# A new order for the opening and the hand-over, and gathers issued in twos behind a result

## The chip, the cores and the metric

The kernel runs on one core of one Trainium2 chip. The metric is the device time of one execution in microseconds (us). Three runs of the kernel before took 702.27, 704.57 and 707.97 us; the median is 704.57 us.

The core has five engines with a queue of instructions each: TensorE (PE; its weight loads are shown as PEld), VectorE (DVE), ScalarE (ACT), GpSimd (POOL) and SyncE (SP), which here only starts transfers. Sixteen DMA engines move the data.

## The reference

Attention within hash buckets, and a mixture of experts behind it (numpy, float32):

```python
q_bucket = sum((q @ proj > 0) * 2**bit); k_bucket likewise      # 4 batches, 8 heads, 768 tokens, 64 wide
scores   = q @ k.T / sqrt(64), -1e9 where the buckets differ
x        = softmax(scores) @ v            # 3072 tokens of 512
logits   = x @ w_gate;  e = argmax(logits)            # 8 experts
out[tok] = softmax(logits)[e] * sigmoid(x @ w_output_gate)[e] * (relu(x @ w1[e]) @ w2[e])
```

The products are made in three float32r parts (high x high, low x high, high x low), so each operand comes as a high tile and a low tile (`xh`/`xlo`, `hh`/`hl`, `w1h`/`w1l`).

## The kernel before, in words

**Attention.** The work runs in 192 steps of a query tile of one head. A step makes scores (TensorE, `ps_s`), clamps them and takes the row extreme (VectorE), exponentiates (ScalarE), divides by the row sum (GpSimd), transposes and multiplies with `v`. The order on each engine is the order of the code: whole blocks are planned by step with `plan` and `block`. `first_heads` (from line 596) is the opening: it splits the first two heads' `q` and `k` into high and low parts before any scores can start. SP writes each head's halves and its bucket bits into place (`spread`).

**Routing and hand-over.** The last batch's routing runs on VectorE beside the first products of the *leading* expert, the fullest one up to then: `fill(f)` makes one of eight slices of relu(x w1) for that expert's first 256 rows, `low()` its low part. `add_pair` adds the last heads' logits, `best`/`choose`/`ranks`/`hot`/`table`/`entries` make the table of which token stands at which place of which expert. With it `lead_slots` and `indices` give row numbers.

**Gathers.** Row numbers go to GpSimd, which starts *indirect* DMAs: `gather` fetches 128 whole rows (`xg`, line 324), `gather_part` a quarter (`xq`, line 365: 128 pieces of 512 bytes), `scatter` writes 128 result rows (line 424). The list `parts` holds the quarter gathers that are still to be issued; `gather_some(m)` issues the next m. An `xq` tile has 4 buffers.

**Experts.** For each expert in order of size (index r, from 0, the leading one), `up` makes two slices at a time: 24 products into one of two `ps_s` buffers, then ScalarE's relu writes `hh` (line 404) and VectorE writes `hl` (line 405); the buffer is free for the next but one slice after that. Then come the products with w2 (`all_rows` or `down`). The turned rows of the next expert are prepared meanwhile (`turned`: VectorE transposes `xq` into `xt`, line 374). For r = 0 the rows 0 to 255 have been worked on ahead (`EARLY`), so its loop takes rows 256 to 511 (`x0`, filled by two `turn` calls).

The order of the engines' queues follows the code, except that pieces of the second recorded region (from line 1310) can be drawn into gaps of the first.

Of the kernel before, what the change touches and what calls it, by code (L numbers as in the profile page):

```python
# [65 lines left out]
def lsh_attention_then_moe(  # L66
# [452 lines left out]
    with ExitStack() as actx:  # L519
# [76 lines left out]
        def first_heads(t):  # L596

            qk, qh, ql, kh, kl = tiles(0, 0)
            qk1, qh1, ql1, kh1, kl1 = tiles(0, 1)
            bb = bits_of(0, 0)  # L600
            first = slice(0, HS)
            pp = ps_m.tile([P, HS], F32, name="ps_m")
            for m in range(2):
                nc.tensor.matmul(pp[m * D:(m + 1) * D], pj[:, 0:D], qk[:, m * HS:(m + 1) * HS], start=True, stop=True)
            nc.scalar.copy(kh, qk[:, KEYS])
            nc.vector.tensor_scalar(qh[DOWN, KEYS], qk[UP, first], -0.125, 0.0, ALU.mult, ALU.add)
            nc.scalar.activation(qh[:, first], qk[:, first], AF.Copy, scale=-0.125)
            signed(t)
            nc.gpsimd.tensor_scalar(kh1, qk1[:, KEYS], 1.0, 0.0, ALU.mult, ALU.add)
            nc.vector.tensor_tensor(kl, qk[:, KEYS], f32(kh), ALU.subtract)  # L610
            nc.scalar.activation(qh1[:, first], qk1[:, first], AF.Copy, scale=-0.125)
            bt = hp.tile([P, HS], BF16, name="bt", bufs=2)
            nc.vector.tensor_scalar(bt, pp, 0.0, set0, ALU.is_gt, ALU.is_equal)
            nc.vector.scalar_tensor_tensor(ql[:, first], qk[:, first], -0.125, f32(qh[:, first]),
                                           ALU.mult, ALU.subtract)
# [4 lines left out]
            for h in range(2):  # L620
                r = D + 32 * h
                nc.gpsimd.tensor_scalar(bb[h * D:h * D + 2 * NB, S:S + HS], bt[r:r + 2 * NB], 1.0, 0.0,
                                        ALU.mult, ALU.add)
            project(0, ps_a.tile([P, HS], F32, name="ps_a"), (1,))

            for n in range(2):
                for h in range(2):
                    c = (n ^ h) * HS
                    nc.scalar.activation(bb[h * D:h * D + 2 * NB, c:c + HS], bt[32 * n:32 * n + 2 * NB],
                                         AF.Copy, scale=PEN)  # L630
            nc.gpsimd.tensor_tensor(kl1, qk1[:, KEYS], f32(kh1), ALU.subtract)
            for m in (1, 0):
                spread_bits(0, 1, m)
            for h in (1, 0):
                spread_bits_half(0, 1, h)

        def second_low():
            split_lo(0, 1, 0)
            for h in (1, 0):
                spread_half(0, 1, h)  # L640
# [14 lines left out]
        def split_late(j):  # L655
            st = pairs[1]
            q = gp.tile([P, S // 32, 32], F32, name="xb", bufs=1).rearrange("p a b -> p (a b)")[:, 0:HS]
            nc.gpsimd.tensor_scalar(q, st["qk"][j][:, 0:HS], -0.125, 0.0, ALU.mult, ALU.add)
            nc.gpsimd.tensor_tensor(st["ql"][j][:, 0:HS], q, f32(st["qh"][j][:, 0:HS]), ALU.subtract)
# [145 lines left out]
        def routing(b):  # L805
# [28 lines left out]
            def add_pair(hf, i):  # L834
                pm = ps_m.tile([P, 3, 32], F32, name="ps_m")
# [134 lines left out]
        for g in range(NP):  # L970
# [15 lines left out]
            elif g == 1:  # L986
                plan(0, lambda: split_hi(1, 0), lambda: split_lo(1, 0, 1, nc.gpsimd))
                plan(2, second_low, lambda: load_v(0), lambda: load(2))
# [75 lines left out]
        def order():  # L1064
# [14 lines left out]
            for i in range(1, E):  # L1079
                load_expert(idi, i)  # L1080
            for i in (0, 2, 1):
# [80 lines left out]
        with tc.manual_schedule(engines=MANUAL | {mybir.EngineType.SP}):  # L1162
            t = signs()
# [16 lines left out]
            turn_idle(12)  # L1180
            first_heads(t)
            turn_idle(1)
# [32 lines left out]
            for s in range(PER, NSTEP + LAG, 2):  # L1215
                k = s % PER
                both = range(s, s + 2)
                for x in both:
                    if x < NSTEP:
                        live[x] = scores(x)  # L1220
                        raw.append(x)
                    if x == PER:
                        project(1)
# [48 lines left out]
            low()  # L1272
            r["add_pair"](1, lp)
# [4 lines left out]
            rows(NP - 1, 1, False)  # L1278
# [14 lines left out]
            r["table"]()  # L1293
            low()
            r["entries"]()
            gid0 = lead_slots(EARLY)
# [3 lines left out]
    with tc.manual_schedule(engines=MANUAL):  # L1300
        pick = slot_picks()
        xg = [gather(gid0[:, a:a + 1]) for a in range(EARLY)]
        order()
        gid, sid = indices(mp, tacc)
        xgs = {(1, a): (gather(gid[:, 1, a:a + 1])[0], chunks(1)[a]) for a in range(WHOLE)}
# [16 lines left out]
        for a in range(WHOLE, NCH):  # L1322
            fetch(a, 1)
        x0 = new_x0()
        for c in range(EARLY):
            py = ps_s.tile([P, 2, 512], F32, name="ps_s")[:, 0]
            for f in range(0, NFB, 2):
                down_rows(c, CH, w2s, hs, py, [f, f + 1])
                if c and f in (2, 4):
# [9 lines left out]
        for r in range(E):  # L1339
# [29 lines left out]
            for fp in range(NFB // 2):  # L1369
# [6 lines left out]
                split()  # L1376
                gather_some(2)
# [5 lines left out]
            def hook(k, a, cc):  # L1383
# [8 lines left out]
                gather_some(2)  # L1392
# [123 lines left out]
```

## Time and profile before

| | us |
|---|---|
| median of three runs | 704.57 |
| the profiled execution | 704.21 |
| its span, first to last instruction | 702.4 |
| TensorE busy in the span | 681.2 |
| VectorE, ScalarE, GpSimd busy | 475.1, 434.6, 414.9 |

All times of rows are from the start of the span. "Idle before" is how long the engine stood still before a row, and the name behind the arrow is what ended it; "issue" means nothing that the profile shows, "remote" an event that it can't put to an engine of the core. Of a row of products the length is modelled, so their pace is read from the distance of their starts.

### The profile page before, as it was taken

Reading aid. Unit: us, or ns where it says so; the run is one execution under the profiler, and the core shown is the slowest. Engines: PE = TensorE matmul, PEld = TensorE weight load, DVE = VectorE, ACT = ScalarE, POOL = GpSimd, SP = SyncE. Lnnn points to the kernel's source line nnn. Section 1 sums busy time; section 2 is a strip of 40 time slices with the busy share of each in tenths; the row PEclk is TensorE's granted clock in tenths of the full one; section 3 lists DMA queues with packets and bytes.
Section 4 is the critical chain, followed back from the end, with each engine's and each line's share of the span. In section 5 each row is a group of like instructions: output and inputs, shape, how many; then the busy total and the mean of one; then the engine's idle time right before and its main releaser. Section 6 shows DMA issues by size and latency. Waiting matters only on the chain. (4 is left out here: it accounts for less than half of the span.)

```text
span 702.4 us, 17340 instructions
## 1 busy us (share of the span) xinstructions
PE 681.2 (97%) x6537; PEld 540.3 (77%) x6537; DVE 475.1 (68%) x1058; ACT 434.6 (62%) x889; POOL 414.9 (59%) x553
## 2 busy tenths in 40 slices
PE   8999999999999999999999968999999999899997
PEld 4667676766766676767676958889999999888996
DVE  6878887889887888878878704563747464545640
ACT  6788998889888988898985112531515252343241
POOL 5877766577756778567985473444272727274003
PEclk9999999999999999999999987999999999999999
DMA  4644454354434444424453223734657576665332
GB/s 145 176 122 102 128 129 97 80 136 120 108 108 96 119 109 123 122 60 90 133 176 67 71 70 113 247 109 146 217 188 248 191 229 201 190 216 185 132 90 84
DMA packets 96724, 96.07 MB, mean 137 GB/s; under 512 B 57967, under 2 KB 76967, under 8 KB 96632
## 3 DMA queue, kind: packets, MB, share of 16 engines
q1 hardware_dynamic: 79704, 72.88, 36.9%
q0 software_dynamic: 5312, 13.25, 5.3%
q10 hardware_dynamic: 11616, 8.75, 4.3%
q8 instruction: 54, 0.88, 0.5%
q14 instruction: 38, 0.31, 0.1%
HBM read 63.77 MB, written 17.50 MB: 116 GB/s over the span
## 5 line engine op out<-in xcount | busy, mean ns | idle before, releaser
L725 POOL TENSOR_SCALAR sc<-sc,rsum 128x768 f32<-128x768 f32 x191 | 170.9, 911 | 77.3 <-ACT pts L761 37.5
L706 DVE TENSOR_SCALAR_CACHE_REDUCE sc<-ps_s 128x768 f32<-128x768 f32 x192 | 176.4, 954 | 23.2 <-PE ps_s L703 21.9
L714 ACT ACTIVATE sc<-sc,mn 128x768 f32<-128x768 f32 x192 | 178.8, 951 | 2.9 <-DVE sc L706 2.7
L703 PE MATMUL ps_s<-kh,qhl 64*128 64x384 f32 x768 | 149.2, 403 | 0.5 <-DMA qhl<-qhl 0.5
L404 ACT ACTIVATE hh<-ps_s 128x256 fp32r<-128x256 f32 (+8 forms) x40 | 29.1, 727 | 173.2 <-PE ps_s L394 96.2
L772 PE MATMUL ps_a<-pts,vt 128*64 128x384 f32 x768 | 131.2, 491 | 0.0
L365 POOL DMA_INDIRECT xq<-x_dram,idx x86 | 91.5, 1064 | 33.3 <-issue 23.8
L761 ACT COPY pts<-ps_t 128x384 f32<-128x384 f32 x188 | 92.8, 495 | 24.2 <-PE ps_s L754 21.0
L394 PE MATMUL ps_s<-xh,w1h 128*128 128x256 f32 (+7 forms) x288 | 98.3, 341 | 9.5 <-DVE hl L405 9.3
L772 PEld LDWEIGHTS ps_a<-pts,vt 128*64 128x64 f32 x768 | 52.4, 137 | 66.8 <-issue 61.5
L394 PE MATMUL ps_s<-xh,w1l 128*128 128x256 f32 (+7 forms) x288 | 97.2, 337 | 1.7 <-issue 1.7
L394 PE MATMUL ps_s<-xlo,w1h 128*128 128x256 f32 (+7 forms) x288 | 97.4, 338 | 0.7 <-issue 0.7
L754 PEld LDWEIGHTS ps_t<-ident,sc 64*128 64x128 f32 x1140 | 81.8, 138 | 20.3 <-POOL sc L725 10.8
L405 DVE SCALAR_TENSOR_TENSOR hl<-ps_s,hh 128x256 fp32r<-128x256 f32 (+8 forms) x40 | 33.9, 848 | 92.6 <-ACT hh L404 73.3
L754 PE MATMUL ps_t<-ident,sc 64*128 64x64 f32 x1140 | 86.7, 223 | 0.0
L703 PEld LDWEIGHTS ps_s<-kh,qhl 64*128 64x128 f32 x768 | 76.6, 189 | 1.6 <-DMA qhl<-qhl 0.8
L394 PEld LDWEIGHTS ps_s<-xh,w1h 128*128 128x128 f32 x288 | 55.9, 194 | 14.0 <-DVE hl L405 10.9
L703 PE MATMUL ps_s<-kl,qhl 64*128 64x384 f32 x384 | 66.6, 334 | 0.0
L703 PE MATMUL ps_s<-bb 64*128 64x384 bf16 x384 | 65.1, 328 | 0.7 <-DMA bb<-bt 0.3
L380 POOL TENSOR_SCALAR xh<-xt 128x512 fp32r<-128x512 f32 (+5 forms) x21 | 11.9, 567 | 82.8 <-DVE xt L374 74.6
L394 PEld LDWEIGHTS ps_s<-xh,w1l 128*128 128x128 f32 x288 | 55.8, 194 | 2.7 <-issue 1.6
L394 PEld LDWEIGHTS ps_s<-xlo,w1h 128*128 128x128 f32 x288 | 55.8, 194 | 1.6 <-issue 0.5
(273 smaller groups left out, 1388.7 us busy)
## 6 DMA issues: line engine op xcount, KB each, us to landing
w_raw<-in_w_dram SPq DMA_DIRECT2D x31, 512.0 KB
qk<-in_qkT_dram SPq DMA_DIRECT2D x32, 384.0 KB
qhl<-qhl SPq DMA_DIRECT2D x62, 192.0 KB
xh<-in_w_dram SPq DMA_DIRECT2D x14, 512.0 KB
xlo<-in_w_dram SPq DMA_DIRECT2D x14, 512.0 KB
vt<-in_v_dram SPq DMA_DIRECT2D x16, 384.0 KB
x_dram<-xb SPq DMA_DIRECT2D x60, 96.0 KB
yt<-y_dram ACTq DMA_DIRECT2D x14, 256.0 KB
```

The lines of the kernel that those rows point to most:

```text
L365: nc.gpsimd.indirect_dma_start(out=xq[:, k * P:(k + 1) * P], out_offset=None, in_=x_dram.rearrange("n (a f) -> (n a) f", a=NB32), in_offse ...
L380: nc.gpsimd.tensor_scalar(xh, w[:, :, 0:n], 1.0, 0.0, ALU.mult, ALU.add)
L394: nc.tensor.matmul(ps, l, r, start=first and k == 0, stop=last and k == len(pairs) - 1)
L404: nc.scalar.activation(hh, ph, AF.Relu)
L405: return lambda: nc.vector.scalar_tensor_tensor(hl, ph, 0.0, f32(hh), ALU.max, ALU.subtract)
L703: nc.tensor.matmul(ss[:, h, 0:HS], q[rs, c:c + P], k[rs, 0:HS], start=(i == 0), stop=(i == 3))
L706: nc.vector.tensor_scalar(sc, ss[:, :, 0:HS], MASKED, None, ALU.min, ALU.min, accum_out=mn)
L714: nc.scalar.activation(pr, pr, AF.Exp, bias=mn, scale=-1.0, accum_out=sums[s // GROUP][:, k, 0:1])
L725: e.tensor_scalar(live[s0 + k], live[s0 + k], rs[:, k:k + 1], 0.0, ALU.mult, ALU.add)
L754: nc.tensor.transpose(trs[h][:, c], pr[r, c * P:(c + 1) * P], ident[r, r])
L761: (nc.vector.tensor_copy if h and s and (last or s % PER == 0 or s in (3, 5)) else nc.scalar.copy)(pts[:, :, t * P + h * hq:t * P + (h + 1 ...
L772: nc.tensor.matmul(st["av"][n * D:(n + 1) * D], st["v"][:, n if g else hf, c], blocks[hb][n][:, c], start=(c == 0), stop=(c == NT - 1))
```

## The change

The opening: TensorE's warm-up runs on a tile of zeros and is split around the first projection; ScalarE and VectorE make the parts of `q` before those of `k`; the low part of the second head's `q`, which VectorE made inside step 2 (`second_low`), is made by ScalarE and GpSimd in the opening. SP starts the bits of a half before its `q` parts, in every pair. The hand-over: the last pair's `add_pair` calls, the low parts of w1 and the last rows' transposes stand later, `low()` of slice 0 earlier, and `table`, `entries` and the row gathers behind the first two w2 products of chunk 0. The gathers: `pace` is a one-element GpSimd copy of a result, so that GpSimd waits until that result is there.

```diff
@@ first_heads
+            turn_idle(2)
+            nc.scalar.activation(qh[:, first], qk[:, first], AF.Copy, scale=-0.125)
+            nc.vector.tensor_scalar(qh[DOWN, KEYS], qk[UP, first], -0.125, 0.0, ALU.mult, ALU.add)
             nc.scalar.copy(kh, qk[:, KEYS])
...
+            q = scaled()
+            nc.scalar.activation(q, qk1[:, first], AF.Copy, scale=-0.125)
+            nc.gpsimd.tensor_tensor(ql1[:, first], q, f32(qh1[:, first]), ALU.subtract)
...
-        def second_low():
-            split_lo(0, 1, 0)
-            for h in (1, 0):
...
@@ spread
             for h in (1, 0):
+                spread_bits_half(g, j, h)
                 spread_half(g, j, h)
-                spread_bits_half(g, j, h)
@@ the opening's warm-up
-            turn_idle(12)
+            for i in range(8):
+                nc.tensor.matmul(idle[:, i % 3], blank, blank, start=True, stop=True)
+            turn_idle(1)
             first_heads(t)
-            turn_idle(1)
@@ hand-over
             for i, (p, hi) in enumerate(zip(w2p, early["w2h"] + [w2_round(ep, p, nc.scalar) for p in w2p[2:]])):
-                if i == 2:
-                    for cc in range(1, NCC):
-                        late_low(cc)
                 w2s += w2_low(ep, p, hi)
+                if i == 0:
+                    low()
             for c in range(NT):
                 weighted(2 * NP - 1, c)
-                if c == 0:
-                    rows(NP - 1, 0, False)
-                if c == 2:
-                    r["add_pair"](0, lp)
+            for cc in range(1, NCC):
+                late_low(cc)
             fill(1)
-            low()
-            r["add_pair"](1, lp)
+            for hf in range(2):
+                r["add_pair"](hf, lp)
...
@@ experts
-        for a in range(WHOLE, NCH):
-            fetch(a, 1)
+        def pace(x):
+            nc.gpsimd.tensor_copy(mp.tile([1, 1], F32, name="tick", bufs=2), f32(x))
+
         x0 = new_x0()
         for c in range(EARLY):
...
                 down_rows(c, CH, w2s, hs, py, [f, f + 1])
+                if c == 0 and f == 0:
+                    r["table"]()
+                    r["entries"]()
+                    gid0 = lead_slots(EARLY)
+                    xg = [gather(gid0[:, a:a + 1]) for a in range(EARLY)]
...
                 if c and f in (2, 4):
                     turn(xg[f // 2 - 1], x0, (f // 2 - 1) * CH)
+                    pace(x0[0][0:1, 0, (f // 2 - 1) * CH:(f // 2 - 1) * CH + 1])
+                    gather_some(2)
             send(0, c, CH, py, sid)
             if c == 0:
                 idx = slot_rows(tacc, pick)
-                gather_some(NCH * EARLY)
+            gather_some(2 - c)
@@ up, of each expert
                 split()
+                if r == 0:
+                    pace(hs[0][0:1, 2 * fp, 0:1])
                 gather_some(2)
@@ down, of each expert
-                gather_some(2)
+                if r or k % 2 == 0:
+                    gather_some(2 if r else 1)
```

GpSimd's queue from the end of the routing table to the middle of the second expert, before (`xg`, `xq`: gathered rows and quarters; `out_dram`: a scatter of results):

```order
L275 TENSOR_TENSOR t_rhs<-t_rhs,t_gl 128x192
L324 DMA xg<-x_dram,gid_8143 128x512 x2
L324 DMA xg<-x_dram,gid 128x512
L424 DMA out_dram<-yo,sid 3072x512
L365 DMA xq<-x_dram,idx 128x128 x8
L424 DMA out_dram<-yo,sid 3072x512
L365 DMA xq<-x_dram,idx 128x128 x13
L424 DMA out_dram<-yo,sid 3072x512
L365 DMA xq<-x_dram,idx 128x128 x4
L424 DMA out_dram<-yo,sid 3072x512
L380 TENSOR_SCALAR xh<-xt 128x4x128 x2
```

The same place now:

```order
L324 DMA xg<-x_dram,gid_8248 128x512 x2
L324 DMA xg<-x_dram,gid 128x512
L424 DMA out_dram<-yo,sid 3072x512
L365 DMA xq<-x_dram,idx 128x128 x2
L1325 COPY tick<-xh_8226 1x1
L365 DMA xq<-x_dram,idx 128x128 x2
L1325 COPY tick<-xh_8226 1x1
L365 DMA xq<-x_dram,idx 128x128 x2
L424 DMA out_dram<-yo,sid 3072x512
L365 DMA xq<-x_dram,idx 128x128
L1325 COPY tick<-hh 1x1
L365 DMA xq<-x_dram,idx 128x128 x2
```

The first eight quarter gathers stood in one row, and thirteen behind the second scatter. Now a copy that waits for a turned row (`xh`) or a relu (`hh`) stands after two, two and three of them; behind the last row shown come a copy, two gathers, two copies and four gathers.

VectorE's queue in the hand-over, from the last pair's low parts to the first step of the routing, before (`w1l`, `w2l`: low parts of weights; `lgt`: logits; `ot`: the last heads' result; `xb`: rows on their way to memory):

```order
L226 TENSOR_TENSOR w2l<-w2l,w2h 128x1024 x2
L1132 TENSOR_TENSOR w1l<-w_raw,w1h 128x512 x2
L1132 TENSOR_TENSOR w1l<-w_more,w1h 128x512
L226 TENSOR_TENSOR w2l<-w2l,w2h 128x1024 x2
L795 STREAM_TRANSPOSE xb<-ot 128x384
L840 TENSOR_TENSOR lgt<-lgt,ps_m 128x48
L775 COPY ot<-ps_a 128x384
L405 SCALAR_TENSOR_TENSOR hl<-ps_s,hh 128x256
L840 TENSOR_TENSOR lgt<-lgt,ps_m 128x48
```

and now:

```order
L226 TENSOR_TENSOR w2l<-w2l,w2h 128x1024
L405 SCALAR_TENSOR_TENSOR hl<-ps_s,hh 128x256
L226 TENSOR_TENSOR w2l<-w2l,w2h 128x1024 x3
L777 COPY ot<-ps_a 128x384
L1138 TENSOR_TENSOR w1l<-w_raw,w1h 128x512 x2
L1138 TENSOR_TENSOR w1l<-w_more,w1h 128x512
L843 TENSOR_TENSOR lgt<-lgt,ps_t 128x48
L843 TENSOR_TENSOR lgt<-lgt,ps_m 128x48
```

The copy of `ot`, on which the last logits wait, moved ahead of three low parts of w1, a transpose and a sum of logits.

## Rows read from the trace of the kernel before

**Rows 1.** The page: the span, and TensorE's busy time, share and instructions.
```profile
span 702.4 us, 17340 instructions
PE 681.2 (97%) x6537; PEld 540.3 (77%) x6537; DVE 475.1 (68%) x1058; ACT 434.6 (62%) x889; POOL 414.9 (59%) x553
```

**Rows 2.** Waits, whole span: engine, waits for, us in total, times, longest.
```profile
ACT hh L404 <- remote: 77.0, 7, 17.8
```

**Rows 3.** Waits from 400 to 435 us.
```profile
ACT hh L404 <- remote: 16.6, 2, 12.1
PE ps_s L394 <- DVE hl L405: 7.5, 1, 7.5
```

**Rows 4.** Timeline of TensorE, first expert: start, length, line, output and inputs, [idle before].
```profile
408.13 0.28 PE L394 MATMUL ps_s<-xh,w1h 128*128 128x256 f32 x1
...
411.14 0.28 PE L394 MATMUL ps_s<-xh,w1h 128*128 128x256 f32 x1
...
414.71 0.28 PE L394 MATMUL ps_s<-xh,w1l 128*128 128x256 f32 x1 [0.20 <-issue]
422.49 0.58 PE L394 MATMUL ps_s<-xh,w1h 128*128 128x256 f32 x1 [7.50 <-DVE hl L405]
...
432.53 0.40 PE L394 MATMUL ps_m<-w2h,hh 128*128 128x512 f32 x1
```

**Rows 5.** Stretches: us, busy time by engine, granted TensorE clock, DMA share, GB/s.
```profile
415.00:420.00 5.00, 0.00 (x0) 0.00 (x0) 0.00 (x0) 0.00 (x0) 3.78 (x5) 0.62 0.24 80
420.00:426.00 6.00, 2.72 (x12) 2.71 (x13) 0.69 (x1) 0.60 (x1) 2.46 (x3) 0.50 0.14 44
```

**Rows 6.** Timeline of ScalarE: relus of the first, second and fourth expert.
```profile
421.12 0.60 ACT L404 ACTIVATE hh<-ps_s 128x512 fp32r<-128x512 f32 x1 [12.10 <-remote]
426.17 0.60 ACT L404 ACTIVATE hh<-ps_s 128x512 fp32r<-128x512 f32 x1 [4.45 <-remote]
428.96 0.60 ACT L404 ACTIVATE hh<-ps_s 128x512 fp32r<-128x512 f32 x1 [2.20 <-PE ps_s L394]
...
448.97 0.94 ACT L404 ACTIVATE hh<-ps_s 128x928 fp32r<-128x928 f32 x1 [4.38 <-PE ps_s L394]
...
529.02 0.86 ACT L404 ACTIVATE hh<-ps_s 128x832 fp32r<-128x832 f32 x1 [17.83 <-remote]
```

**Rows 7.** Timeline of GpSimd: first and last of the runs of indirect DMAs.
```profile
397.18 1.42 POOL L324 DMA_INDIRECT xg<-x_dram,gid  x1 [3.09 <-DVE gid L1061]
...
410.77 0.94 POOL L365 DMA_INDIRECT xq<-x_dram,idx  x1 [0.30 <-issue]
...
422.12 0.95 POOL L365 DMA_INDIRECT xq<-x_dram,idx  x1 [0.30 <-issue]
432.43 0.94 POOL L365 DMA_INDIRECT xq<-x_dram,idx  x1 [9.36 <-DVE xt L374]
```

**Rows 8.** Timeline of GpSimd, second and fourth expert.
```profile
441.38 1.58 POOL L424 DMA_INDIRECT out_dram<-yo,sid  x1 [1.76 <-issue]
...
511.06 0.31 POOL L380 TENSOR_SCALAR xh<-xt 128x128 fp32r<-128x128 f32 x1
...
527.85 0.96 POOL L424 DMA_INDIRECT out_dram<-yt,sid  x1 [0.30 <-issue]
```

**Rows 9.** Timeline of VectorE, in the fourth expert's down products.
```profile
521.95 0.71 DVE L443 STREAM_TRANSPOSE yb<-ps_m 128x416 f32<-128x416 f32 x2 [3.99 <-PE ps_m L394]
```

**Rows 10.** Waits of TensorE from 0 to 20 us.
```profile
PE ps_t L1178 <- POOL ident masks.py:199: 1.4, 1, 1.4
PE ps_s L703 <- DMA qhl<-qhl: 0.5, 1, 0.5
```

**Rows 11.** Timeline of ScalarE and VectorE, opening: operations like those added and removed.
```profile
5.81 0.52 ACT L611 ACTIVATE qhl<-qk 128x384 fp32r<-128x384 f32 x1 [0.75 <-DMA qk<-in_qkT_dram]
...
13.05 0.56 DVE L650 SCALAR_TENSOR_TENSOR qhl<-qk,qhl 128x384 fp32r<-128x384 f32 x1
```

**Rows 12.** Timeline of TensorE and VectorE, hand-over.
```profile
384.27 0.54 DVE L775 COPY ot<-ps_a 128x384 f32<-128x384 f32 x1
...
384.87 0.85 PE L839 MATMUL ps_m<-wgt,ot 128*128 128x32 f32 x6 [0.67 <-DVE ot L775]
...
387.74 0.57 DVE L795 STREAM_TRANSPOSE xb<-ot 128x384 f32<-128x384 f32 x1
```

More of the change, by code (lines that the diff above doesn't have):

```diff
@@ L619, in first_heads @@
                 nc.sync.dma_start(f32(x)[UP, KEYS], f32(x)[DOWN, first])
[L620 to L623, printed above, removed]
             project(0, ps_a.tile([P, HS], F32, name="ps_a"), (1,))
@@ L635, in first_heads, with scaled @@
                 spread_bits_half(0, 1, h)
-        def second_low():
-            split_lo(0, 1, 0)
-            for h in (1, 0):
                 spread_half(0, 1, h)
+        def scaled():
+            return gp.tile([P, S // 32, 32], F32, name="xb", bufs=1).rearrange("p a b -> p (a b)")[:, 0:HS]
         def split_hi(g, j):
@@ L656, in split_late @@
             st = pairs[1]
-            q = gp.tile([P, S // 32, 32], F32, name="xb", bufs=1).rearrange("p a b -> p (a b)")[:, 0:HS]
+            q = scaled()
             nc.gpsimd.tensor_scalar(q, st["qk"][j][:, 0:HS], -0.125, 0.0, ALU.mult, ALU.add)
@@ L834, in add_pair @@
             def add_pair(hf, i):
-                pm = ps_m.tile([P, 3, 32], F32, name="ps_m")
+                pool, name = (ps_m, "ps_m") if hf else (ps_t, "ps_t")
+                pm = pool.tile([P, 3, 32], F32, name=name)
                 hs = slice(hf * 3, hf * 3 + 3)
@@ L987, in lsh_attention_then_moe @@
                 plan(0, lambda: split_hi(1, 0), lambda: split_lo(1, 0, 1, nc.gpsimd))
-                plan(2, second_low, lambda: load_v(0), lambda: load(2))
+                plan(2, lambda: load_v(0), lambda: load(2))
                 plan(4, lambda: split_late(0))
@@ L1080, in order, with slots @@
                 load_expert(idi, i)
+        def slots():
             for i in (0, 2, 1):
@@ L1162, in lsh_attention_then_moe @@
         with tc.manual_schedule(engines=MANUAL | {mybir.EngineType.SP}):
+            blank = gp.tile([P, S], F32, name="lt")[:, 0:P]
+            nc.gpsimd.memset(blank, 0.0)
             t = signs()
@@ L1218, in lsh_attention_then_moe @@
                 for x in both:
+                    if x == PER:
+                        project(1)
                     if x < NSTEP:
@@ L1221, in lsh_attention_then_moe @@
                         raw.append(x)
-                    if x == PER:
-                        project(1)
                     if x == PER + 1:
@@ L1277, in lsh_attention_then_moe @@
             r["choose"]()
-            rows(NP - 1, 1, False)
+            for hf in range(2):
+                rows(NP - 1, hf, False)
             fill(3)
@@ L1292, in lsh_attention_then_moe @@
             r["hot"]()
-            r["table"]()
             low()
-            r["entries"]()
-            gid0 = lead_slots(EARLY)
             low()
@@ L1301, in lsh_attention_then_moe @@
         pick = slot_picks()
-        xg = [gather(gid0[:, a:a + 1]) for a in range(EARLY)]
         order()
-        gid, sid = indices(mp, tacc)
-        xgs = {(1, a): (gather(gid[:, 1, a:a + 1])[0], chunks(1)[a]) for a in range(WHOLE)}
+        xgs = {}
         parts = []
@@ L1320, in gather_some @@
             del parts[:m]
-        for a in range(WHOLE, NCH):
-            fetch(a, 1)
+        def pace(x):
+            nc.gpsimd.tensor_copy(mp.tile([1, 1], F32, name="tick", bufs=2), f32(x))
         x0 = new_x0()
         for c in range(EARLY):
-            py = ps_s.tile([P, 2, 512], F32, name="ps_s")[:, 0]
+            py = ps_s.tile([P, 2, 512], F32, name="ps_s")[:, 0] if c else ps_a.tile([CH, DM], F32, name="ps_a")
             for f in range(0, NFB, 2):
                 down_rows(c, CH, w2s, hs, py, [f, f + 1])
+                if c == 0 and f == 0:
[3 more added lines that the diff above has]
+                    xg = [gather(gid0[:, a:a + 1]) for a in range(EARLY)]
+                    slots()
+                    gid, sid = indices(mp, tacc)
+                    for a in range(WHOLE):
+                        xgs[1, a] = gather(gid[:, 1, a:a + 1])[0], chunks(1)[a]
+                    for a in range(WHOLE, NCH):
+                        fetch(a, 1)
                 if c and f in (2, 4):
                     turn(xg[f // 2 - 1], x0, (f // 2 - 1) * CH)
+                    pace(x0[0][0:1, 0, (f // 2 - 1) * CH:(f // 2 - 1) * CH + 1])
+                    gather_some(2)
             send(0, c, CH, py, sid)
```

13 lines of the change are left out of this document (7 added, 6 removed).

## The prediction, made before the changed kernel ran

> **What bounds the kernel now.** I read the page first. TensorE is busy 681.2 of 702.4 us [rows 1], so a change pays only where it shortens what TensorE waits for or runs slowly through. I then looked for such places in the list of waits. Over the whole span ScalarE's relus waited 77.0 us for something "remote", in seven cases [rows 2]. Nothing is remote here: the kernel has one core. Two of the seven lie between 400 and 435 us, and beside them stands TensorE's one long wait, 7.5 us for a low part `hl` [rows 3].
>
> TensorE's timeline shows the place [rows 4]. It is the leading expert's loop over rows 256 to 511: four groups of 24 products, from 408.13 to the first w2 product at 432.53, 24.40 us. The first group took 411.14 − 408.13 = 3.01 us; four at that pace are 12.04. So 24.40 − 12.04 = **12.4 us** are lost in this one hole. Its pieces: the second group ended at 414.71 + 0.28 = 414.99, 0.84 late; 7.50 idle; and the last two groups took 432.53 − 422.49 = 10.04 instead of 6.02, 4.02 more. The stretches explain the last piece: the granted clock was 0.50, the 1.2 GHz level, from 420 to 426 us, after 5 us in which TensorE, VectorE and ScalarE did nothing at all [rows 5].
>
> Why did nobody work? The first group's product had ended by 411.14, but its relu started at 421.12, 10.0 late. The second's ended at 414.99, its relu started at 426.17, 11.2 late. The third and fourth relu (428.96, with TensorE named as the releaser) came promptly [rows 6]. In the same time GpSimd started indirect DMAs without a pause, every 1.24 us (0.94 and 0.30), from 397.18 to 422.12 + 0.95 = 423.07, and then stood still for 9.36 us [rows 7]. The late relu at 529.02 follows the last of such a run too, which ended at 527.85 + 0.96 = 528.81 [rows 6, 8]. Where a run is short nothing is late: after a GpSimd pause of 1.76 us before 441.38, the relu at 448.97 came at once [rows 6, 8]; and after a compute operation at 511.06, eight indirect DMAs on, VectorE at 521.95 was released by TensorE at once [rows 8, 9]. My reading: signals to ScalarE come late when GpSimd has issued some eleven indirect DMAs or more without a compute operation or a pause. It rests on coincidence in time; no row shows the mechanism.
>
> **The change part by part.** The sum is made against the profiled execution: 704.21 us, its span of 702.4 and 1.8 around it, 0.36 below the median.
>
> *Gathers in twos.* Nothing is removed: the quarters leave in the same order, but behind copies that wait. Up to the first relu's copy GpSimd now starts three row gathers, two scatters and seven quarters, twelve indirect DMAs. The table stands behind two w2 products now, by my estimate 1.4 us later against the loop's start T0 (408.13 before); so the first gather, T0 − 10.95 before, goes at about T0 − 9.5. Twelve starts of 1.24, and 0.5 more for the first as in [rows 7], end at about T0 + 6. When the first relu is due, at T0 + 3, nine or ten have been started, with two copies between them; since the second copy, only a few. Both ways of counting leave the run short of eleven. So I forecast prompt relus and the hole closed: **−12.4**. Bounds: 0 (nothing closes) and −12.4; a gain above the hole has no place to come from.
>
> A copy of one element costs GpSimd at most what its smallest operation here does, 0.31 us [rows 8]; six are under 2 us, covered by its pause of 9.36 [rows 7]. Behind a waiting copy are queued only gathers and a scatter of finished results; no product waits for that scatter. The quarters after the copies are issued as the relus come, at T0 + 3, 6, 9 and 12. In the trace of before GpSimd resumed at 432.43, T0 + 24.3, when VectorE had emptied a buffer of the first quarters [rows 7]; so the last quarters have some 10 us before they are turned, and the cost is 0. If that cover is gone, the second expert's turned rows are late next, by as much as the gathers slip.
>
> *Opening.* Warm-up on zeros no longer waits for `ident` (1.4 us), and the wait for `qhl` (0.5) should go since the second head's parts leave earlier [rows 10]. VectorE loses one low part of 0.56 in step 2; ScalarE gets a scaled copy of 0.52 and GpSimd a subtraction [rows 11]. The ident wait is filled with blank warm-up work, which nothing needed, and products start when `qk` has landed; I count it at nothing. I take 0.47 + 0.56 = **−1.0**. Bounds: all three, −2.5; and +0.5, if ScalarE's copy stands on the path. The bits ahead of the halves on SP in every pair move transfers by one issue each; the one wait for such a transfer in 0 to 20 us is the 0.5 counted here, so 0 beyond it.
>
> *Hand-over.* TensorE waited 0.67 us for the copy of `ot` at 384.27, which had stood behind the low parts of w1 [rows 12]. It now stands ahead of them, but the last logits stand behind both halves' products, and both transposes of 0.57 fall behind the routing. Bounds −0.67 to +0.57; I take **−0.4**. The table moved behind two w2 products is covered by the six others.
>
> Sum: 704.21 − 12.4 − 1.0 − 0.4 = 690.4, against the median 690.8; I put **690.5**. With the bounds of the small terms (−1.8 to +1.9), a remainder of 0.8 for the issue gap in the second group and one for run to run, the forecast's own range is 688 to 693.
>
> **The rivals.**
>
> *The run is still too long, and a relu is late again (R1).* Twelve starts before the first relu's copy are close to eleven; if an interposed copy doesn't count as a pause, the eleventh falls before the second relu is due. But then the copy that waits for that relu stops GpSimd, and this cuts the lateness short. GpSimd's last gather before the second relu's copy ends at about T0 + 6.5 + 2 × 1.24 = T0 + 9. The relu followed the end of a run by 0.2 (528.81 to 529.02) to 3.1 us (423.07 to 426.17) [rows 6 to 8], so it starts at T0 + 9.2 to 12.1. With 0.60 for it and some 0.8 for `hl`, the fourth group, due at T0 + 9.0, waits 1.6 to 4.5; if the clock falls, one or two groups cost up to 4.0 more. Loss 1.6 to 8.5, so 692 to 699; its centre **696**. Against it: the copies are compute operations, and at 511.06 one ended a run [rows 8].
>
> *The change doesn't do what it says (R2).* The late relus may have another cause, and gathers and relus only share the period after a table. Then the hole stays: 704.21 − 1.0 − 0.4 = **702.8**. For it: while the relus were late, DMA engines were busy only 24% and 14% [rows 5], so no transfer was crowded. Against it: long runs and late relus coincide twice in [rows 6 to 8], and short runs and prompt ones twice.
> A rule speaks for R2: the Trainium skill, "SBUF — State Buffer", section "SBUF: two separate sides", says that engine ports and DMA ports are disjoint, that a DMA cannot be slowed by a compute operation nor the reverse, and that the engine side contends only at the pair shared by GpSimd and VectorE. By that rule, gathers cannot hold back a relu and the time would be 702.8; the trace agrees as to bytes (0.24 and 0.14), and disagrees as to the 10.0 and 11.2 us, unless something other than a port delays a signal.
>
> *Gathers in flight are enough, not a long run (R3, the other side).* Then pacing spreads the harm: before, the third relu fell into GpSimd's silence [rows 6, 7]; now two to four gathers leave around every one of the four. The first two stay late and the last two join, each by 3.1 (the smaller lag above) to 10.0 us: 702.8 + 2 × 3.1 = **709** to 702.8 + 2 × 10.0 = 723. It decides as soon as a relu is late behind four or fewer gathers. Against it: the relu at 448.97 came at once with five since the pause [rows 6, 8].
>
> **How the numbers follow.** Forecast 0.45, R1 0.28, R2 0.18, R3 0.09. The time is the forecast's, 690.5. The range goes from 687.5 (half a us under the forecast's own, for run to run) to 702.5, which takes in R1 whole and the lower part of R2; left out are R3, more than half of R2 and the edges, about 0.2. One per cent, 7 us, is about what can be told from no change here. Faster by more (under 697.5): the forecast and three quarters of R1, 0.66. Within it: the rest of R1, R2 and the near part of R3, 0.07 + 0.18 + 0.04 = 0.29. Slower (over 711.6): 0.05.
>
> **What the changed profile would show.** Right: from the first product of that loop to its first w2 product about 12 us; no "remote" wait at its four relus, each within 1 us of its group's end; granted clock 1.00 there; GpSimd's copies released by the relus, not the reverse; `qhl` gone from the waits of the opening, and `ot` from those of the hand-over. R1: one late relu, and a hole of 1.6 to 8.5 us. R2: relus some 10 us late, though GpSimd stands at a copy the while. R3: four late relus. The later late relus, such as 529.02, should stand as before, since their runs of gathers are unchanged or longer. What would make the prediction wrong: a count other than about eleven that decides, or quarters so late that the second expert waits for its rows.

## The result and the profile after

The changed kernel took 696.79 us (median of six runs, 693.92 to 699.93) against 704.17 us for six runs of the kernel before: a ratio of 0.9886, 95% interval 0.986 to 0.9911. It is faster by 1.1%. The time lies in the predicted range, 6 us above the predicted figure and near the centre of the rival R1. Timed again later, beside the experiments, it took 690.81 against 700.79 us, a ratio of 0.9857 (0.9813 to 0.9902). That this second figure equals the forecast of 690.5 is luck: the kernel before was 3.4 us faster there as well, and the drop was 10.0 us where the forecast had 13.8.

The page of the changed kernel, and its longest waits over the whole span, against [rows 1] and [rows 2]:

```profile
span 696.2 us, 17349 instructions
PE 680.0 (98%) x6543; PEld 541.0 (78%) x6543; DVE 474.4 (68%) x1058; ACT 435.3 (63%) x890; POOL 417.0 (60%) x560
```

```profile
ACT hh L404 <- remote: 32.1, 4, 18.7
```

Four relus instead of seven still wait for the unnamed event. One of them stands in the leading expert's loop. The waits from 395 to 435 us, against [rows 3]:

```profile
POOL tick L1325 <- ACT hh L404: 7.4, 3, 3.5
ACT hh L404 <- remote: 7.2, 1, 7.2
```

TensorE in that loop, against [rows 4]:

```profile
404.66 0.28 PE L394 MATMUL ps_s<-xh,w1h 128*128 128x256 f32 x1
...
407.67 0.28 PE L394 MATMUL ps_s<-xh,w1h 128*128 128x256 f32 x1
...
410.57 0.28 PE L394 MATMUL ps_s<-xlo,w1h 128*128 128x256 f32 x1
411.18 0.28 PE L394 MATMUL ps_s<-xh,w1l 128*128 128x256 f32 x1 [0.33 <-issue]
411.89 0.38 PE L394 MATMUL ps_s<-xh,w1h 128*128 128x256 f32 x1 [0.43 <-issue]
412.62 0.39 PE L394 MATMUL ps_s<-xlo,w1h 128*128 128x256 f32 x1 [0.34 <-issue]
412.84 0.28 PE L394 MATMUL ps_s<-xh,w1l 128*128 128x256 f32 x1
414.14 0.58 PE L394 MATMUL ps_s<-xh,w1h 128*128 128x256 f32 x1 [1.02 <-DVE hl L405]
...
423.11 0.39 PE L394 MATMUL ps_m<-w2h,hh 128*128 128x512 f32 x1
```

The loop takes 423.11 − 404.66 = 18.45 us, against 24.40 before and 12.04 without loss. The 7.50 us of standing still have become 1.02, but the second group, begun at 407.67, ended only at 413.12. And the clock still falls, for less time; against [rows 5]:

```profile
410.00:415.00 5.00, 2.42 (x10) 1.65 (x10) 1.29 (x2) 1.08 (x2) 1.56 (x3) 0.84 0.17 66
415.00:420.20 5.20, 5.20 (x27) 5.20 (x26) 0.00 (x0) 0.53 (x1) 3.43 (x5) 0.50 0.17 47
```

ScalarE's relus (against [rows 6]; the first row holds two of them) and GpSimd (against [rows 7]):

```profile
412.76 1.08 ACT L404 ACTIVATE hh<-ps_s 128x512 fp32r<-128x512 f32 x2 [7.21 <-remote]
419.67 0.60 ACT L404 ACTIVATE hh<-ps_s 128x512 fp32r<-128x512 f32 x1 [5.82 <-issue]
...
423.36 0.59 ACT L404 ACTIVATE hh<-ps_s 128x512 fp32r<-128x512 f32 x1
```

```profile
394.59 1.08 POOL L324 DMA_INDIRECT xg<-x_dram,gid  x1 [2.59 <-DVE gid L1064]
...
403.09 0.18 POOL L1325 COPY tick<-xh 1x1 f32<-1x1 f32 x1
...
405.65 0.18 POOL L1325 COPY tick<-xh 1x1 f32<-1x1 f32 x1
...
409.83 0.97 POOL L365 DMA_INDIRECT xq<-x_dram,idx  x1 [0.31 <-issue]
413.49 0.18 POOL L1325 COPY tick<-hh 1x1 f32<-1x1 f32 x1 [2.68 <-ACT hh L404]
```

The first relu was due at 407.83, when the last of 24 products ended, and came at 412.76, 4.93 us late: 1.96 us after GpSimd's last gather had ended (410.80) and GpSimd stood at the copy. The two copies that wait for turned rows did not wait: both rows have no idle time before them. So only the copies that wait for relus made GpSimd stand still. The other three relus came within 0.2 us of their products' ends, though the second one's products had themselves ended late.

The opening and the hand-over. The last bias product of the scores (TensorE, timeline, before and after) tells when attention ends; then TensorE's one remaining wait for another engine in 0 to 20 us (against [rows 10]), and VectorE's copy of `ot`, after which TensorE waits for nothing (against [rows 12]):

```profile
364.87 0.34 PE L703 MATMUL ps_s<-bb 64*128 64x384 bf16 x2
```

```profile
362.57 0.34 PE L705 MATMUL ps_s<-bb 64*128 64x384 bf16 x2
```

```profile
PE ps_t L1189 <- POOL lt L1170: 1.1, 1, 1.1
```

```profile
379.90 0.55 DVE L777 COPY ot<-ps_a 128x384 f32<-128x384 f32 x1
```

With these rows the difference of the two spans divides like this. The second pair is the same reading of two later traces, the changed kernel again and the kernel before again (rows below); they were taken on two different chips.

```
                                         first pair           second pair        predicted
attention's end (last bias product)      364.87 -> 362.57     362.88 -> 362.08
  change                                 -2.30                -0.80              -1.0
from there to the loop's first product   43.26 -> 42.09       43.29 -> 42.08
  change                                 -1.17                -1.21              -0.4
the loop                                 24.40 -> 18.45       23.86 -> 17.05
  change                                 -5.95                -6.81              -12.4
from its end to the span's end           269.87 -> 273.09     267.77 -> 266.89
  change                                 +3.22                -0.88               0
sum                                      -6.20                -9.70              -13.8
```

The first line holds more than the change. In all fourteen traces the first bias product starts somewhere between 7.41 and 9.41 us, with the change or without. From the first bias product to the last it takes 355.07 to 355.60 us in the five traces with the old opening and 354.04 to 354.28 in the nine with the new one: 1.1 us less in the mean. The second line is steady: 43.23 to 43.29 us in the five, 42.06 to 42.09 in the nine.

The last line but one is the later experts. Their late relus come and go from trace to trace: the second relu of the second expert was 3 us late in the first trace of the changed kernel and prompt in the repeat,

```profile
447.48 0.95 ACT L404 ACTIVATE hh<-ps_s 128x928 fp32r<-128x928 f32 x1 [5.12 <-remote]
```

```profile
442.63 0.95 ACT L404 ACTIVATE hh<-ps_s 128x928 fp32r<-128x928 f32 x1 [2.16 <-PE ps_s L394]
```

(first trace, then repeat). This one relu cost little: the second expert's up stage took 20.58 us against 20.21. Of the 8.07 us between the two profiled spans of the changed kernel, 6.17 lie behind the loop, most of it (4.8) in the up stages of the fourth to seventh expert.

### The profile page after: what moved, and what is told of

Same layout as the page of the kernel before. It is cut to its first block, busy times and chain, and to the rows that moved or that the text cites. A ratio compares the mean times of both kernels' runs of the same rounds, so it can differ in the third digit from the quotient of the medians.

```text
span 696.2 us, 17349 instructions
## 1 busy us (share of the span) xinstructions
PE 680.0 (98%) x6543; PEld 541.0 (78%) x6543; DVE 474.4 (68%) x1058; ACT 435.3 (63%) x890; POOL 417.0 (60%) x560
## 3 DMA queue, kind: packets, MB, share of 16 engines
q1 hardware_dynamic: 79704, 72.88, 37.8%
HBM read 63.77 MB, written 17.50 MB: 117 GB/s over the span
## 4 chain that ended last, share of the span: by engine, by line
PE 83%; issue 5%; another core or an unknown queue 4%; DVE 3%; ACT 3%; POOL 1%; DMA 0%; ACTq 0%; POOLq 0%; DVEq 0%
PE ps_s L705 19%; PE ps_a L774 18%; PE ps_s L394 16%; PE ps_t L756 8%; PE ps_m L394 6%; PE ps_t L394 5%; PE ps_a L394 4%; PE ps_t L581 2%; PE ps_m L756 1%; PE ps_m L820 1%; PE ps_a L756 1%; ACT hh L404 1%; DVE hl L405 1%; PE ps_t L1189 1%
```

## The experiments

Twelve runs were made in three groups, two of them repeats; runs of the kernel before stood beside each group (700.74, 700.79 and 699.58 us). A loop is read from one profiled execution of a run, a time is the median of all.

**Without pacing.** The opening and hand-over alone.

```diff
-                    pace(x0[0][0:1, 0, (f // 2 - 1) * CH:(f // 2 - 1) * CH + 1])
-                    gather_some(2)
...
-            gather_some(2 - c)
+                gather_some(NCH * EARLY)
...
-                if r == 0:
-                    pace(hs[0][0:1, 2 * fp, 0:1])
...
-                if r or k % 2 == 0:
-                    gather_some(2 if r else 1)
+                gather_some(2)
```

> The changed kernel with its opening and hand-over, but with the quarter gathers issued as in the kernel before (no copies that wait; eight in a row, then thirteen). Theory A, a long run of GpSimd's indirect DMAs makes signals late and the pacing shortened it: the leading expert's loop takes about 24 us again (24.40 before, 18.45 changed), and the time is 704.2 less what opening and hand-over gave in the traces (2.3 + 1.2), about 700.7. Theory B, the pacing is idle and the loop got shorter because its products moved against something else: loop near 18.5 us, time near 697.

700.06 us, ratio 0.9996 (0.9977 to 1.0016). TensorE's first product and first w2 product of the loop:

```profile
404.32 0.28 PE L394 MATMUL ps_s<-xh,w1h 128*128 128x256 f32 x1
...
428.73 0.39 PE L394 MATMUL ps_m<-w2h,hh 128*128 128x512 f32 x1
```

24.41 us: the hole is back, so the pacing closed what was closed. The expected 700.7 us was met by luck, for the kernel before took 700.74 beside it: opening and hand-over were worth no gain that these runs can tell. The loop does start 1.85 us earlier than that of the repeated kernel before (406.17, on another chip), but in that comparison part was given back: the loop is 0.55 longer, and the rest of the span (697.2 − 428.73) 0.7.

**Pacing alone**, in the kernel before. The four edits above, made the other way round.

> The kernel before with the pacing alone (the waiting copies, quarters in twos), its opening and hand-over untouched. Theory A: the loop takes about 18.5 us and the time is 704.2 - 6 = 698. Theory B: the loop stays near 24.4 us, the time near 704.

689.15 us, ratio 0.9834 (0.9808 to 0.9861): the whole gain, and more than was expected. TensorE and ScalarE:

```profile
406.58 0.28 PE L394 MATMUL ps_s<-xh,w1h 128*128 128x256 f32 x1
...
419.50 0.39 PE L394 MATMUL ps_m<-w2h,hh 128*128 128x512 f32 x1
```

```profile
411.83 0.60 ACT L404 ACTIVATE hh<-ps_s 128x512 fp32r<-128x512 f32 x1 [4.36 <-remote]
```

The loop took 12.92 us. Its first relu was late too, but by 2.09 us, and TensorE lost only 0.9. Why the same twelve starts cost 2.09 us here and 4.93 in the changed kernel is not settled.

**No quarter before the first relu.**

```diff
-                    pace(x0[0][0:1, 0, (f // 2 - 1) * CH:(f // 2 - 1) * CH + 1])
-                    gather_some(2)
...
-            gather_some(2 - c)
...
-                if r or k % 2 == 0:
-                    gather_some(2 if r else 1)
+                gather_some(2)
```

> The changed kernel with no quarter gather before the first relu of the leading expert's loop: the two copies that wait for turned rows and the seven quarters around them are taken out there and the quarters follow behind the four relu copies. GpSimd then issues only three row gathers and two scatters before that relu. Theory A: all four relus within 1 us of their products, loop 12 to 13 us, time 696.8 - 6 = 691 if the second expert's rows still come in time, up to 697 if they do not. Theory B (late relus do not come from the gathers): the first relu is late as before, loop 18 us or more, time 697 or more.

693.63 us, ratio 0.9911 (0.9884 to 0.9937). The loop took 12.03 us and all four relus came within 0.4 us. But the second expert's first product came 3.0 us late, and its up stage took 23.8 instead of 20.2 us:

```profile
431.19 0.75 PE L394 MATMUL ps_s<-xh,w1h 128*128 128x464 f32 x1 [3.04 <-issue]
```

The time lies in the expected range of 691 to 697. The prediction's cover for the last quarters (some 10 us) does not hold seven more of them.

**The rows read by SyncE.** On top of the run without pacing:

```diff
-                gather_part(xgs[e, a][0], idx[:, k, e, a:a + 1], k)
+                if e == 1:
+                    at = (a * NB32 + k) * P
+                    nc.sync.dma_start(out=xgs[e, a][0][:, k * P:(k + 1) * P],
+                                      in_=x_dram.rearrange("n (a f) -> (n a) f", a=NB32)[at:at + P])
+                else:
+                    gather_part(xgs[e, a][0], idx[:, k, e, a:a + 1], k)
```

> As the run without pacing, but the second expert's quarters are read by SyncE with plain transfers of the same size (128 pieces of 512 bytes from fixed places, so the second expert gets other rows), in the place where GpSimd issued them. Theory A (it is GpSimd's issuing): no late relu in the loop, 12 to 13 us, time 12 us below the run without pacing, less what SyncE's later weight loads lose. Theory C (the small pieces in flight are enough, whoever issues them): loop 18 to 24 us. Theory B: as the run without pacing.

686.01 us, ratio 0.9795 (0.9769 to 0.9821), loop 12.03 us. The stretch from 404 to 417 us without pacing and with SyncE's rows (columns as in [rows 5]):

```profile
404.00:417.00 13.00, 6.49 (x51) 5.88 (x49) 0.45 (x2) 1.28 (x2) 9.65 (x12) 0.94 0.21 67
```

```profile
404.00:417.00 13.00, 13.00 (x106) 12.66 (x105) 4.27 (x6) 3.62 (x7) 5.26 (x6) 1.00 0.12 42
```

TensorE was busy for 6.49 of 13 us beside twelve GpSimd DMAs, and for all 13 beside six. The time fell by 14.05 us against the run without pacing, 12.38 of it in the loop. R2 falls. Theory C (pieces in flight, whoever issues them) is not decided by it: SyncE had no row numbers to wait for and read the rows 30 us earlier.

```profile
371.94 6.01 SPq L1323 DMA_DIRECT2D xq<-x_dram  x11
```

**The changed kernel again**, unedited, and the same with its table back in front of the w2 products:

> The changed kernel once more, beside the three below, because the pacing alone gave 689.2 us with a loop of 12.92 us, while the changed kernel took 696.8 with a loop of 18.45 when it was first timed. Theory D (opening, hand-over or the later table spoil the pacing): the loop is near 18.5 us again and the time 4 to 7 us above the pacing alone. Theory E (how late the relus are differs from execution to execution or chip to chip): the loop is between 12 and 16 us and the time 687 to 691.

690.81 us, ratio 0.9857 (0.9813 to 0.9902); the loop:

```profile
362.08 0.34 PE L705 MATMUL ps_s<-bb 64*128 64x384 bf16 x2
...
404.16 0.28 PE L394 MATMUL ps_s<-xh,w1h 128*128 128x256 f32 x1
...
421.21 0.40 PE L394 MATMUL ps_m<-w2h,hh 128*128 128x512 f32 x1
```

The first relu was 4.74 us late (4.93 in the first trace), the loop 17.05 us. Theory D stands for the loop, and falls for the time, which is only 1.7 us above the pacing alone. Theory E has the time right and the loop (12 to 16 us) wrong.

```diff
             r["hot"]()
+            r["table"]()
             low()
+            r["entries"]()
+            gid0 = lead_slots(EARLY)
             low()
...
-                if c == 0 and f == 0:
-                    r["table"]()
...
```

> The changed kernel with table, entries and the row gathers back in their place before the first w2 product of chunk 0 (the rest of the change stays). The row gathers then start some 0.9 us earlier against the loop. Theory D with the later table as the cause: loop near 12.9 us, time 689.2 - 2 (opening and hand-over) = 687. Theory D with another part as the cause, or theory E: loop and time as the changed kernel beside it.

690.35 us, ratio 0.9839 (0.978 to 0.9897), loop 18.26 in the slowest of four executions (688.10, 688.11, 692.58 and 694.18 us). The edit did not do what was expected of it: its row gathers began 9.56 us before the loop, later than the 10.07 of the changed kernel and not earlier, and not the 10.94 of the pacing alone. So it does not show whether the place of the table keeps the loop long.

**Copies for later experts**, on top of the pacing alone:

```diff
-                if r == 0:
+                if r in (0, 5, 6):
                     pace(hs[0][0:1, 2 * fp, 0:1])
```

> The kernel before with the pacing, and copies that wait for the relus of the sixth and seventh expert (r = 5 and 6) as well, the two whose up stages still lose 1.9 to 3.8 and 2.2 us against their down stages. Theory A: their late relus go, up stages of about 17.6 and 16.2 us instead of 18.96 and 18.30, time 689.2 - 3 = 686. Against it: if the copies hold GpSimd's casts of turned rows, the next expert's rows come late and nothing is gained.

688.91 us, ratio 0.9837 (0.979 to 0.9884), against 0.9834 without them: no difference that can be told. The sixth expert's up stage came down to 17.56 us, as expected, but traces without these copies have 17.50 too. The seventh expert's stayed at 18.29 us. There the run in front of the late relu is mostly scatters of results, issued before the first copy.

**Copies that wait for nothing.**

```diff
-            nc.gpsimd.tensor_copy(mp.tile([1, 1], F32, name="tick", bufs=2), f32(x))
+            nc.gpsimd.tensor_copy(mp.tile([1, 1], F32, name="tick", bufs=2), tacc[0:1, 0, 0, 0:1])
```

> The changed kernel with its copies in the same places, but reading one element of the table that is long there, so that they wait for nothing. The prediction's reading (a compute operation between gathers ends a run): loop as in the changed kernel beside it. Theory A' (only a pause of GpSimd ends it, the copy by itself does nothing): loop near 24 us and time near the run without pacing, 700.

699.31 us, ratio 0.9986 (0.9964 to 1.0008), loop 26.24 us. GpSimd and ScalarE:

```profile
410.62 0.18 POOL L1325 COPY tick<-tacc 1x1 f32<-1x1 f32 x1
...
413.20 0.18 POOL L1325 COPY tick<-tacc 1x1 f32<-1x1 f32 x1
```

```profile
414.43 0.60 ACT L404 ACTIVATE hh<-ps_s 128x512 fp32r<-128x512 f32 x1 [9.07 <-remote]
423.65 0.60 ACT L404 ACTIVATE hh<-ps_s 128x512 fp32r<-128x512 f32 x1 [8.62 <-remote]
```

A compute operation between gathers does nothing by itself. The whole worth of the pacing is that GpSimd stands still.

**Fewer starts before the first relu: nine, seven, and nine in the kernel before.**

```diff
-            gather_some(2 - c)
...
                     pace(hs[0][0:1, 2 * fp, 0:1])
-                gather_some(2)
+                gather_some(2 if r else 3)
```

> The changed kernel with the three quarters taken out that were issued behind the results of chunks 0 and 1; they follow in threes behind the relu copies. Nine indirect DMAs instead of twelve are issued before the copy that waits for the first relu, and GpSimd stops some 3.8 us earlier. Theory F (what counts is how many have been issued when the first relu is due; ten were too many): first relu prompt, loop 12 to 13 us, time 690.8 - 4.5 = 686. Theory G (any gathers around the relu delay it until GpSimd has stood still for about 2 us): first relu still 1 to 2 us late, loop near 15, time 689.

688.71 us, ratio 0.9828 (0.9774 to 0.9882), loop 13.55. Theory F holds for the first relu, 0.10 us after its product, and fails for the loop; G fails for the first relu. Now the second is late, by 3.21 (the row of two):

```profile
407.27 0.60 ACT L404 ACTIVATE hh<-ps_s 128x512 fp32r<-128x512 f32 x1 [2.37 <-issue]
413.24 1.09 ACT L404 ACTIVATE hh<-ps_s 128x512 fp32r<-128x512 f32 x2 [5.37 <-PE ps_s L394]
```

For seven, the two quarters behind the second turned row are taken out as well:

> As the run with nine, with seven before the first relu's copy. Theories F and G both have a prompt first relu and a loop of 12 to 13 us; the second expert's rows come later: if the up stage or the turn of the second expert grows by more than 1 us, the optimum lies at nine. Time 686 to 688.

690.41 us, ratio 0.9838 (0.9785 to 0.989), loop 12.03. Three prompt relus, and the fourth 5.25 us late, behind the loop's last product; the second expert starts 2.3 us later for it, and the time misses the expected 686 to 688.

```profile
421.15 0.60 ACT L404 ACTIVATE hh<-ps_s 128x512 fp32r<-128x512 f32 x1 [4.94 <-remote]
```

> The kernel before with the pacing alone, nine indirect DMAs before the first relu's copy. Its loop was 12.92 with twelve, so at most 0.9 can be won: loop 12.0, time 688.3. If the opening and hand-over of the changed kernel are worth the 1.9 us by which its loop starts earlier, the run with nine and the whole change is 1.9 us faster than this one.

690.41 us, ratio 0.9859 (0.9806 to 0.9912), loop 12.12: first relu prompt, second 1.79 and fourth 2.83 late. The loop is as expected, the time 2.1 us above it. The run with nine and the whole change is 1.7 us faster in the median, as expected, but the intervals overlap.

**The kernel before again:**

> The kernel before, for a trace from the same chip: loop of 24.4 us again; its start shows what opening and hand-over gave apart from the chip (3.47 us between the first two traces, 1.9 us between the paced ones).

699.59 us, one run.

```profile
362.88 0.34 PE L703 MATMUL ps_s<-bb 64*128 64x384 bf16 x2
...
406.17 0.28 PE L394 MATMUL ps_s<-xh,w1h 128*128 128x256 f32 x1
...
430.03 0.39 PE L394 MATMUL ps_m<-w2h,hh 128*128 128x512 f32 x1
```

**All loops together.** From the timelines of the fourteen traces: how many indirect DMAs GpSimd had started since the first row gather when a relu's last product ended, and how many us later the relu started.

```
                     relu 1       relu 2       relu 3      relu 4      loop us
before               11,  9.82    14, 11.18    20, 0.04    21, 0.04    24.40
before, again        11,  6.30    13, 11.94    20, 0.04    21, 0.04    23.86
without pacing       10,  8.87    13, 12.53    20, 0.04    21, 0.08    24.41
idle copies          10,  6.80    12, 13.17    20, 0.04    20, 0.04    26.24
changed              10,  4.93    12,  0.14    16, 0.04    16, 0.08    18.45
changed, again       10,  4.74    12,  1.64    16, 0.04    16, 0.09    17.05
table back           10,  4.33    12,  0.04    16, 0.04    16, 0.09    18.26
pacing alone         11,  2.09    12,  0.81    15, 0.04    16, 1.01    12.92
nine                  9,  0.10    11,  3.21    12, 0.86    15, 0.04    13.55
nine, pacing alone    9,  0.10    11,  1.79    12, 0.54    15, 2.83    12.12
seven                 7,  0.10     9,  0.04    11, 0.04    13, 5.25    12.03
none before           5,  0.10     7,  0.04     9, 0.04    11, 0.36    12.03
later copies         11,  2.10    12,  0.80    15, 0.04    16, 0.29    12.92
SyncE's rows          6,  0.10     8,  0.04     9, 0.04    10, 0.21    12.03
```

With nine starts or fewer, all ten relus came within 0.1 us. With ten or eleven, eleven of fourteen were late by 1.8 to 9.8 us. But this does not show that ten is the number that counts, because each of the ten prompt ones also has a stop of GpSimd of 2.0 us or more among its starts. Counted anew from each such stop, the table falls into three parts. All 22 relus with five starts or fewer came within 0.21 us. Seven more came within 0.14 us with GpSimd standing still for 2.3 us or more. Of the other 27, with six starts or more, 25 were late by 0.29 to 13.2 us; the two that were not (the third of the pacing alone and of the later copies) stand behind a stop of 1.6 us. The 2.0 us were chosen after the fact, and the rule does not carry over: in the second expert the first relu came within 0.10 us in eight traces with 8 to 22 starts since such a stop. That a stop of GpSimd ends the lateness is shown; from how many starts it begins is not.

## Why the prediction was right, and where it was not

**The hole, −12.4.** The place and the lever were right: without pacing 24.41 us, with it 12.92 to 18.45. The size failed, at the step "Both ways of counting leave the run short of eleven". Two assumptions in it were wrong. A copy between gathers does not end a run (idle copies: 26.24 us), and staying below eleven is not enough: the changed kernel had started ten when the first relu was due, as the step itself counted ("nine or ten"), and that relu was 4.93 us late; with nine and seven, later relus were late by 3.21 and 5.25 us. The term measures −5.95 and −6.81.

**R1** is what happened, with one difference: the first relu is the late one, not the second (in the repeat both, by 4.74 and 1.64 us). Its mechanism, that the copy which waits for the late relu stops GpSimd and so cuts the lateness short, is shown by the waiting copies against the idle ones (second relu 1.64 against 13.17 us late, loop 17.05 against 26.24). Its lag of 0.2 to 3.1 us after GpSimd's last gather held the measured 1.96, and its price of 1.6 to 8.5 us the measured 6.4 (18.45 − 12.04).

**R2** fell: with the second expert's gathers moved away from GpSimd no relu of the loop is late, and the times are 696.79 and, with the rows read by SyncE, 686.01, not 702.8. The Trainium skill, "SBUF — State Buffer", section "SBUF: two separate sides", says that a DMA cannot be slowed by a compute operation nor the reverse. Here products were held up beside GpSimd's DMAs all the same (6.49 busy of 13 us); no run shows two accesses meeting at a port, and what is late in the traces is TensorE's semaphore updates (last section).

**R3** fell: the changed kernel's third relu came within 0.1 us with four gathers just before it, and with none before the first relu the second and third came so with two and four. One relu speaks for it, the fourth of the pacing alone: 1.01 us late behind four gathers, if the stop of 1.6 us before them counts.

**Opening, −1.0.** −2.30 in the first pair, −0.80 in the second; 1.1 less from the first bias product to the last, over all traces, so the size was about right. It comes within the first 48 bias products (36.6 to 36.7 us in three traces with the change, 37.8 to 38.0 in three without). The wait for `qhl` (0.5) is gone; the wait for `ident` has become 1.1 us for the tile of zeros, and another of 0.6, for `pjc`, is gone as well. Which edit gave the rest is not shown: the second projection now also stands behind the first scores, and one half's bits moved from GpSimd to VectorE, which no term priced.

**Hand-over, −0.4.** −1.17 and −1.21, beyond the bound of −0.67. The wait for `ot` was sized too small: 0.67 us counts from a modelled end. By the starts, the first product with `ot` came 0.94 us after the last product before it (383.93 to 384.87 in [rows 12]); now it follows by 0.12, the pace of the products around it:

```profile
383.93 0.28 PE L394 MATMUL ps_s<-xh,w1l 128*128 128x256 f32 x1
```

```profile
380.71 0.28 PE L394 MATMUL ps_s<-xh,w1l 128*128 128x256 f32 x1
380.83 0.75 PE L842 MATMUL ps_t<-wgt,ot 128*128 128x32 f32 x6
```

That is 0.82 us. Some 0.38 more is the time from start to start of the 48 products with `v` and the twelve with `ot`, 9.67 us before and 9.29 now; the first half's six no longer stand among those with `v`, a loss that no term had. A weight load's wait can mislead here (kernel before):

```profile
379.64 0.74 PEld L839 LDWEIGHTS ps_m<-wgt,ot 128*128 128x128 f32 x6 [0.60 <-DVE w2l L226]
382.51 0.19 PEld L394 LDWEIGHTS ps_s<-xh,w1h 128*128 128x128 f32 x1 [0.60 <-issue]
```

The 0.60 put down to `w2l` cost nothing: a load stands idle as long at 382.51, where it waits for no engine, and in both places the product starts 0.42 us after the last one with `v`.

**What no term had:** what the later experts' late relus do, +3.22 in one trace and −0.88 in the other. The prediction said that they would stand as before; they move by more than the opening and the hand-over are worth. Without pacing those two show no gain that can be told (ratio 0.9996, 0.9977 to 1.0016).

**Slips in the working.** The first relu's "10.0 late" counts from 411.14, the next group's start; from its own product's end, 411.30, it is 9.82. The bounds of the small terms add up to +2.5 (0.5 + 1.0 and 0.57 + 0.4), not +1.9. The first row gather went at T0 − 10.07, not T0 − 9.5. None of these changes which rival came out.

**What stays open.** Why a signal comes late behind GpSimd's indirect DMAs, why the first relu is 2.1 us late in the pacing alone and 4.7 to 4.9 in the changed kernel after the same twelve starts, and whether transfers of the same size from another queue, at the same moment, would do the same. Every run on record carries a span and a granted clock, so none shows the kernel without that recording. The run with nine and the pacing alone (ratios 0.9828 and 0.9834) are the fastest apart from the one with other rows; they cannot be told from the repeat of the changed kernel (0.9857).

## What to carry to other kernels

When an engine waits for something that the profile cannot name, line up every late start with what the other engines were issuing, and look for the last long pause, not for the last operation. A pacing copy helps only by making the issuer stand still, so put it where the issuer has not yet started too much, and check that what it holds back is not needed soon after. Before pricing a small wait, compare the distances of the products' starts: idle time of a weight load can cost nothing, and idle time after a modelled end can be too short.

## What the hardware showed that was not expected

Inside one group of 24 products, where the profile shows no wait for another engine, TensorE's starts fell from 0.12 us apart to 0.6 to 0.7 us (410.57, 411.18, 411.89, 412.62 in the changed kernel), while the first relu's signal was held up; both ended together at 412.8. So it is not ScalarE that is held.

The traces' record of semaphore updates says the same. In the kernel before, the updates that release the first two relus are recorded at 421.04 and 426.15 us, and the relus started 0.08 and 0.02 us later. Over all fourteen traces up to 670 us, with each update put down to the last instruction of its semaphore that had ended (which can hide a late one), 92 came more than 0.5 us late (at most 13.14), and all 92 are TensorE's. Of some 25 400 updates of the other engines none came more than 0.1 us late, not even the 31 that fell into the stretches in which TensorE's were outstanding. TensorE's ends are modelled, so whether its last product or only the signal of it is late is not shown.

The granted clock fell to 0.50 (the 1.2 GHz level) behind these stalls, as in the kernel before, and the last two groups took 423.11 − 414.14 = 8.97 us instead of 6.02.
